# Attention and a gated MLP on one core: the opening of the program is put into another order, its first products are split by head block, and five scalings move to GpSimd

## The chip, the core and the metric

The kernel runs on one core of one Trainium2 chip. A core has TensorE (PE, matmuls; its weight loads are shown as PEld), VectorE (DVE), ScalarE (ACT), GpSimd (POOL) and SyncE (SP), each with its own instruction stream, and DMA engines that move data between the chip's main memory and SBUF, the working memory on the core. Matmuls write to PSUM, eight banks of 128 partitions by 512 float32 values. The metric is the device time of one execution in microseconds (us); lower is better.

## What is computed

```
# x [8, 8, 512, 64], state [8, 8, 32, 64]: batch, heads, rows, depth
scores  = softmax(x @ state^T / 8)          # 512 x 32 for each batch and head
xread   = scores @ state                    # 512 x 64
scores2 = softmax(state @ x^T / 8)          # 32 x 512
sread   = scores2 @ x                       # 32 x 64
X = concat([xread, sread], rows) -> [8 * 544, 512]      # the heads side by side
out = (relu(X @ w_gate) * (X @ w_val)) @ w_out          # 512 -> 1536 -> 512
```

All inputs and the output are float32; the kernel multiplies in bfloat16. It doesn't form xread. Since xread @ w = answers @ (state @ w), it works out U = state @ w once for each batch, for the gate and the value weights, and multiplies the normalized answers (512 by 256 for a batch, heads and state rows side by side, in two head blocks of 128) with U.

## The kernel before, in words

**Pieces of work.** A batch has a number b (0 to 7), and its 1,536 hidden columns are 12 pieces jf of 128. For a batch the steps are: cast of x to bfloat16 and transposes on TensorE (`x_T`, L162) with copies out of PSUM (`x_out`, L165); scores with the state (`att_sc`, L179), exponentials on ScalarE (`att_exp`, L206), row sums and reciprocals on VectorE (`att_sum`, L212 and L214), the scaling a = e * (1 / sum) (`att_scale`, L218), the transposes of a (`att_T`, L234) and their copies (`att_out`, L248), each for head block 0 and 1. U is built in units: `c_unit` (L298, for batches 0 and 1, 128 or 256 columns of gate and value together) or `u_unit` (512 columns of one of them), and cast into SBUF (`c_out` L320, `u_out` L310). A product `gv` (L325) of one piece jf is four matmuls of 512 columns: gate and value, each summed over the two head blocks in one PSUM bank. `relu` (L354, ScalarE) and `mult` (L358, VectorE) make the hidden piece h, and the output matmuls (L367) sum the 12 pieces of h with w_out. The sread rows go through `sr_mm`, `gvs` and `fin_s`.

**Order.** The scheduler of the framework is off (`manual_schedule`, L412): every engine runs its instructions in the order in which the code names them. Up to piece 28 (all 12 pieces of batches 0 and 1, the first four of batch 2) the order is a written list, the string `program` (L455): each word is a step with its arguments, digits behind @ are the PSUM banks that it takes, and a last part act, dve or pool is the engine of a copy, cast or scaling. From piece 28 on a loop (L554) sets one piece of a product and one piece of an output row block in turn, with further work at fixed places. Only the list is in question here; the loop is the same in both kernels.

**Words of the list.** dw and dx load weights and x, ds the state, do the output weights, all on GpSimd's queue. spin and spin32 are matmuls on constants into a bank that nobody reads, in bfloat16 and float32; they keep TensorE busy while it has nothing to do. stc, stT and sto cast, transpose and copy the state; xc casts the half of the first x that is loaded as float32; xT and xo are transposes and copies; sc, ex, nr, nx, aT, ao the attention steps; c and co (u and uo) U's units and casts; gv a whole product, re and mu relu and multiplication; xp copies x into a padded tile for the sread rows. Words ga, gb, wa and wb (one matmul of a product: gate or value, head block 0 or 1) and gg and gw (gate alone, value alone) are defined and not used.

**Queues.** GpSimd's loads use eight semaphores in turn, so the ninth load is issued only when the first has landed. A load stands in GpSimd's stream like any other of its instructions; it is issued when what stands ahead of it is done. Two small loads at the start go out on SyncE's and ScalarE's queues (L420 and L99).

Of the kernel before, what the change touches and what calls it, by code (L numbers as in the profile page):

```python
# [16 lines left out]
def kernel(  # L17
# [9 lines left out]
    nc = tc.nc  # L27

    B, H, S, D = x.shape
# [34 lines left out]
    xa = const.tile([128, NX, NC * H, DP], BF16, name="xa")  # L64
# [4 lines left out]
    stT = const.tile([128, 2, B, H, Ns], BF16, name="stT")  # L69
# [4 lines left out]
    warm32 = nc.const_aps.tensor(1.0, (128, 512), FP32)  # L74
# [3 lines left out]
    xf, xb, xT, eT, e_sn, a_sn, ANS, U, hsb = {}, {}, {}, {}, {}, {}, {}, {}, {}  # L78
# [359 lines left out]
    def spin(n, cols=512, src=warm):  # L438
        for i in range(n):
            nc.tensor.matmul(warm_ps[:, 0:cols], src[:, 0:128], src[:, 0:cols], start=True, stop=True)  # L440
# [3 lines left out]
    def x_load_behind(b, gb, gj):  # L444
# [1 line left out]
        nc.gpsimd.tensor_copy(out=mark, in_=held["g", gb, gj][:, 0:1])  # L446
        x_load(b, 0, 1)

    steps = {"spin32": lambda n: spin(n, 512, warm32), "dxb": x_load_behind, "spin": spin, "stc": state_conv, "stT": state_T, "sto": state_out, "xc": x_conv_pair, "xT": x_T, "on": lambda: nc.gpsimd.memset(xa[:, :, :, D:D + 1], 1.0), "dw": w_load, "dx": x_load, "ds": lambda: state_dma(nc.gpsimd, 2, B), "do": wo_dma,
             "xo": x_out,   # L450
             "sc": att_sc, "ex": att_exp, "nr": att_sum, "nx": att_scale, "aT2": att_T2, "ao2": att_out2, "aT": att_T, "ao": att_out,
             "c": c_unit, "co": c_out, "u": u_unit, "uo": u_out, "gv": gv, "gg": lambda b, jf: g_part(b, jf, 0, (0, 1)), "gw": lambda b, jf: g_part(b, jf, 1, (0, 1)),
             "ga": lambda b, jf: g_part(b, jf, 0, (0,)), "gb": lambda b, jf: g_part(b, jf, 0, (1,)), "wa": lambda b, jf: g_part(b, jf, 1, (0,)), "wb": lambda b, jf: g_part(b, jf, 1, (1,)), "re": relu, "mu": mult, "o": out_part,
             "of": fin_x, "xd": x_trans_dma, "ad": att_aT_dma, "xp": x_pad, "sr": lambda b: sr_mm((b,)), "sn": lambda b: sr_norm((b,))}
# [10 lines left out]
    nx.1.1 aT.1.0@4 aT.1.1@6 c.0.256.256@01 co.1.0.128.0.dve ao.1.0.dve c.1.256.256@57 co.0.256.256.0.act  # L465
    co.1.256.256.0.act co.1.256.256.1.act ao.1.1.dve co.0.256.256.1.dve gv.1.0@46 re.1.0 mu.0.0 mu.0.1 gv.0.2@01
    gv.1.2@53 mu.1.0 re.0.2 c.0.512.256@72 c.1.512.256@40 re.1.2 mu.1.2 co.0.512.256.1.dve mu.0.2 gv.1.3@65
    gv.1.1@32 co.1.512.256.1.act re.1.3 co.0.512.256.0.act re.1.1 co.1.512.256.0.dve gv.0.3@06 gv.1.5@17 mu.1.1
    mu.1.3 re.0.3 re.1.5 gv.1.4@34 mu.0.3 c.0.768.256@02 re.1.4 mu.1.5 c.0.1024.256@51 c.1.768.256@63
    co.0.768.256.0.act co.0.768.256.1.act mu.1.4 co.1.768.256.1.dve co.1.768.256.0.dve gv.0.4@74 gv.0.6@02 re.0.4  # L470
    co.0.1024.256.0.act re.0.6 gv.0.7@37 co.0.1024.256.1.dve mu.0.4 re.0.7 mu.0.6 gv.1.7@65 mu.0.7 re.1.7
    c.0.1280.256@10 c.1.1024.256@43 c.1.1280.256@26 mu.1.7 co.1.1280.256.1.act co.0.1280.256.0.act
    co.0.1280.256.1.dve co.1.1024.256.1.act co.1.1280.256.0.dve gv.0.9@75 co.1.1024.256.0.act gv.0.8@60 gv.0.5@12
    re.0.5 re.0.9 xT.2.0.8@3 re.0.8 mu.0.5 xT.2.8.8@4 xo.2.0.8.dve stT.1@1 sto.1.1.act xo.2.8.8.dve sto.1.0.act
    gv.0.11@72 re.0.11 mu.0.11 mu.0.8 gv.1.9@63 gv.1.11@41 re.1.9 mu.1.9 gv.0.10@76 gv.1.6@20 re.1.11 re.0.10
    sc.2.1@4 gv.1.10@73 re.1.10 ex.2.1 re.1.6 mu.0.10 mu.0.9 o.0.3@6 sc.2.0@5 o.0.4 ex.2.0 o.0.0@7 mu.1.10 mu.1.11
    u.2.1.1024@43 mu.1.6 nr.2.1 uo.2.1.1024.1.act u.2.1.0@21 u.2.1.512@50 uo.2.1.512.1.act uo.2.1.1024.0.act
    uo.2.1.512.0.act uo.2.1.0.0.act nx.2.1 uo.2.1.0.1.dve o.0.1 o.0.5 stc.2.1.pool dx.3.0.1 xp.1 xp.0 sr.1@3
    stc.3.0.pool nr.2.0 sr.0@0 nx.2.0 sn.1 u.2.0.0@14 ad.2 xd.3 of.0.1.act u.2.0.1024@52 u.2.0.512@63 o.0.2 of.0.0.act
    uo.2.0.0.0.act uo.2.0.512.1.act uo.2.0.512.0.dve o.0.6@6 o.0.7 o.0.9@7 o.0.8 of.0.2.act sn.0 gv.1.8@01  # L480
    uo.2.0.0.1.dve uo.2.0.1024.0.dve gv.2.0@45 re.1.8 mu.1.8 re.2.0 mu.2.0 dxb.4.2.0 gv.2.2@36 xp.3 gv.2.3@40 re.2.2 mu.2.2 re.2.3 mu.2.3 xp.2
    gv.2.1@31 re.2.1 mu.2.1 uo.2.0.1024.1.act
    """
    for word in program.split():
        word, _, banks = word.partition("@")
# [117 lines left out]
```

## Time and profile before

| | us |
|---|---|
| time, median of 3 runs | 220.07 (219.66 to 220.4) |
| the profiled execution's own time | 219.39 |
| its span in the profile | 217.6 |
| TensorE busy | 212.8 |
| VectorE busy | 135.0 |
| ScalarE busy | 117.8 |
| GpSimd busy | 42.5 |

The span is the time from the first to the last instruction that the profile shows; the rest of the execution's own time lies around it. A busy time says how long an engine had an instruction under way. The chain of work that ended last goes back from the last instruction to what released it, and so on to the start. A line of a timeline gives start and busy time in us, engine, source line, operation, tile written and tiles read, shapes and count, and in brackets how long the engine stood idle before and who ended that.

### The profile page before, as it was taken

Reading aid. Unit: us, or ns where it says so; the run is one execution under the profiler, and the core shown is the slowest. Engines: PE = TensorE matmul, PEld = TensorE weight load, DVE = VectorE, ACT = ScalarE, POOL = GpSimd, SP = SyncE. Lnnn points to the kernel's source line nnn. Section 1 sums busy time; section 2 is a strip of 40 time slices with the busy share of each in tenths; the row PEclk is TensorE's granted clock in tenths of the full one; section 3 lists DMA queues with packets and bytes.
Section 4 is the critical chain, followed back from the end, with each engine's and each line's share of the span. In section 5 each row is a group of like instructions: output and inputs, shape, how many; then the busy total and the mean of one; then the engine's idle time right before and its main releaser. Section 6 shows DMA issues by size and latency. Waiting matters only on the chain.

```text
span 217.6 us, 4865 instructions
## 1 busy us (share of the span) xinstructions
PE 212.8 (98%) x1952; PEld 104.8 (48%) x1952; DVE 135.0 (62%) x233; ACT 117.8 (54%) x225; POOL 42.5 (20%) x63
## 2 busy tenths in 40 slices
PE   8899999999999999999999999999999999999994
PEld 4554454454444444444444444444544445666543
DVE  4799967956887678557966796388745444222100
ACT  4798877747546556455555656454646443333221
POOL 7974049005600531020107000000000000000000
PEclk9999999999999999999999999999999999999999
DMA  7999999579963995919491453131311122222132
GB/s 168 180 196 197 202 221 171 78 139 188 152 175 74 144 186 110 167 52 193 99 148 60 110 134 96 49 99 50 84 28 51 48 48 50 61 56 80 51 96 96
DMA packets 47399, 24.96 MB, mean 115 GB/s; under 512 B 27824, under 2 KB 43056, under 8 KB 47376
## 3 DMA queue, kind: packets, MB, share of 16 engines
q0 software_dynamic: 16896, 9.05, 31.0%
q1 hardware_dynamic: 29584, 14.85, 28.7%
q10 hardware_dynamic: 896, 0.75, 1.3%
q8 instruction: 15, 0.25, 0.4%
q14 instruction: 8, 0.07, 0.2%
HBM read 18.35 MB, written 8.91 MB: 125 GB/s over the span
## 4 chain that ended last, share of the span: by engine, by line
PE 96%; DVE 1%; ACT 1%; issue 0%
PE o_ps L367 40%; PE gv_ps L325 38%; PE gv_ps L347 5%; PE up L298 4%; PE warm_ps L440 2%; PE upc L298 2%; PE o_ps L396 1%; PE sr_ps L265 1%; PE sc_ps L179 1%; PE sT_ps L189 1%; PE xT_ps L162 1%; ACT e_sn L206 1%; DVE xT L165 1%; ACT xT L165 0%; PE aT_ps L234 0%; DVE cs L212 0%
## 5 line engine op out<-in xcount | busy, mean ns | idle before, releaser
L367 PE MATMUL o_ps<-wo_sb,h_sb 128*128 128x512 bf16 x372 | 94.3, 379 | 0.0
L325 PE MATMUL gv_ps<-ans,U 128*128 128x512 bf16 x384 | 93.2, 379 | 0.0
L358 DVE TENSOR_TENSOR h_sb<-gv_ps,g_sb 128x512 bf16<-128x512 f32 x96 | 65.1, 688 | 42.8 <-ACT g_sb L354 41.3
L354 ACT ACTIVATE g_sb<-gv_ps 128x512 bf16<-128x512 f32 (+1 forms) x108 | 61.7, 578 | 51.4 <-PE gv_ps L325 39.1
L325 PEld LDWEIGHTS <-U 128*128 128x128 bf16 x384 | 37.1, 98 | 44.5 <-issue 0.8
L367 PEld LDWEIGHTS <-h_sb 128*128 128x128 bf16 x372 | 35.2, 98 | 42.0 <-issue 4.0
L310 DVE CAST U<-up 128x512 bf16<-128x512 f32 x44 | 27.7, 684 | 5.7 <-PE up L298 5.7
L375 ACT COPY o_sb<-o_ps 128x512 f32<-128x512 f32 x31 | 18.4, 594 | 19.7 <-PE o_ps L367 17.7
L310 ACT CAST U<-up 128x512 bf16<-128x512 f32 x28 | 14.7, 595 | 8.8 <-PE up L298 8.8
L254 POOL COPY xa<-xb 128x1024 bf16<-128x1024 bf16 x16 | 16.0, 1045 | 10.0 <-PE sr_ps L265 5.9
L358 DVE TENSOR_TENSOR hs_sb<-gv_ps,g_sb 128x256 bf16<-128x256 f32 x12 | 5.1, 425 | 15.3 <-PE gv_ps L347 10.4
L212 DVE TENSOR_REDUCE cs<-e_sn 128x16 f32<-128x512 bf16 x16 | 10.8, 677 | 1.1 <-ACT e_sn L206 1.1
L218 DVE TENSOR_TENSOR a_sn<-e_sn,rc 128x512 bf16<-128x512 bf16 x16 | 10.9, 687 | 0.4
L298 PEld LDWEIGHTS <-stT 64*32 64x32 bf16 x560 | 6.7, 91 | 6.4 <-issue 5.3
L320 ACT CAST U<-upc 128x512 bf16<-128x512 f32 (+1 forms) x19 | 8.7, 522 | 1.7 <-PE upc L298 1.7
L446 POOL COPY mark<-g_sb 128x1 bf16<-128x1 bf16 x4 | 0.8, 190 | 41.8 <-ACT g_sb L354 41.8
L197 ACT ACTIVATE eT<-sT_ps 128x512 bf16<-128x512 f32 x10 | 5.4, 594 | 5.3 <-PE sT_ps L189 5.3
L434 POOL DMA_DIRECT2D xb<-in_x_dram x8 | 6.8, 847 | 3.1 <-DMA wg_sb<-in_moe_w_gate_dram 1.4
L347 PE MATMUL gv_ps<-br,wg_sb 128*128 128x256 bf16 x48 | 7.2, 273 | 0.0
L347 PE MATMUL gv_ps<-br,wv_sb 128*128 128x256 bf16 x48 | 7.2, 273 | 0.0
L399 DVE COPY o_sb<-o_ps 128x64 f32<-128x64 f32 x2 | 0.4, 224 | 10.6 <-PE o_ps L396 10.5
L298 PE MATMUL up<-wg_sb,stT 64*32 64x512 bf16 (+1 forms) x168 | 6.9, 348 | 0.0
(59 smaller groups left out, 124.1 us busy)
## 6 DMA issues: line engine op xcount, KB each, us to landing
out_dram<-o_sb SPq DMA_DIRECT2D x26, 256.0 KB, 2.4
xb<-in_x_dram POOLq DMA_DIRECT2D x6, 512.0 KB, 7.1
wo_sb<-in_moe_w_out_dram POOLq DMA_DIRECT2D x2, 768.0 KB, 10.5
out_dram<-o_sb SPq DMA_DIRECT2D x11, 128.0 KB, 2.4
wg_sb<-in_moe_w_gate_dram POOLq DMA_DIRECT2D x5, 256.0 KB, 9.4
wv_sb<-in_moe_w_val_dram POOLq DMA_DIRECT2D x5, 256.0 KB, 10.0
xb<-in_x_dram POOLq DMA_DIRECT2D x3, 256.0 KB, 5.3
st_f<-in_state_dram POOLq DMA_DIRECT2D x1, 384.0 KB, 11.4
```

The costliest lines, as they stand in the source:

```text
L212: nc.vector.reduce_sum(out=cs, in_=e_v, axis=AX.X)
L218: {"dve": nc.vector, "pool": nc.gpsimd}[eng].tensor_tensor(out=a_sn[b][:, jp].rearrange("p c (j n) -> p c j n", n=Ns), in0=e_v, in1=held[" ...
L254: nc.gpsimd.tensor_copy(out=v[:, hs], in_=xb[b][:, hs])
L298: nc.tensor.matmul(dst[kc][i0:i0 + 32], stT[r:r + 64, parity, b, h], wsb[r:r + 64, j, lo:lo + n], start=True, stop=True)
L310: copy[eng](out=U[b][:, w, kc, lo:lo + 512], in_=held["u", b, w, lo][kc])
L320: copy[eng](out=U[b][:, :, kc, lo:lo + n], in_=held["c", b, lo][kc])
L325: nc.tensor.matmul(ps[w], U[b][:, w, kc, f0:f0 + 128], ANS[b][:, kc].rearrange("p c t -> p (c t)"), start=(kc == 0), stop=(kc == NK - 1))
L347: nc.tensor.matmul(ps[w][:, 0:nt], wsb[:, j, f0:f0 + 128], br[:, j].rearrange("p b n -> p (b n)"), start=(j == 0), stop=(j == NJ - 1))
L354: nc.scalar.activation(out=g_sb[:, 0:n], in_=ps[0][:, 0:n], func=AF.Relu)
L358: nc.vector.tensor_tensor(out=dst, in0=ps[1][:, 0:n], in1=held["g", b, jf][:, 0:n], op=ALU.mult)
L367: nc.tensor.matmul(held["o", b, tsub], src[:, jf, tsub * 128:(tsub + 1) * 128], wo_sb[:, jf], start=(jf == 0), stop=(jf == NF - 1))
L375: copy[eng](out=o_sb, in_=held["o", b, tsub])
```

## The change

Almost all of it is the list. Its new order issues the same computation, with these differences:

- The first product matmuls of batches 0 and 1 (pieces 0 to 3) are split into ga, wa, gb and wb, the part over head block 0 ahead of the part over head block 1, with other work between them. The other pieces of the list are split into gg and gw. The number and size of the product matmuls stay the same.
- Five scalings (batch 0, both blocks; batch 1, block 0; batch 2, both blocks) go from VectorE to GpSimd.
- The loads of the weights stand among the other words: the value weights of columns 512 to 767 behind the first two scalings, the further ones behind the third and partly behind the padding copies of batch 1. The order of the loads among themselves stays as it was, but the second half of the output weights now follows the first half directly.
- Fillers: 2 float32 matmuls of 512 columns at the start become one of 512 and one of 320; eight bfloat16 fillers of 128 to 512 columns become six float32 ones of 64 to 512 columns. `spin32` gets a number of columns as second argument.
- Copies and casts change engines in many places: the two casts of the first state pair stand on VectorE and ScalarE instead of both on VectorE, the copies of stT both on VectorE instead of one each.

```diff
-    steps = {"spin32": lambda n: spin(n, 512, warm32), "dxb": x_load_behind, ...
+    steps = {"spin32": lambda n, cols=512: spin(n, cols, warm32), "dxb": x_load_behind, ...
...
     program = """
-    dx.1.0.2 dx.1.1.2 stc.0.1.dve stc.0.0.dve dw.0.0.128 dw.1.0.128 dw.0.128.128 dw.1.128.128 dw.0.256.256
-    dw.1.256.256 dw.0.512.256 spin32.2 stT.0@0 dw.1.512.256 dw.0.768.256 dw.1.768.256 dw.0.1024.256 dw.1.1024.256
-    dw.0.1280.256 dw.1.1280.256 dx.2.0.1 ds do.0.6 xc.0.0.act spin.1.256 xT.0.0.4@1 xc.0.1.dve sto.0.0.act
-    spin.1.128 xT.0.4.4@2 xo.0.0.4.dve sto.0.1.dve xo.0.4.4.act spin.1 sc.0.0@3 ex.0.0 nr.0.0 spin.1.384
-        xT.0.8.4@4 xT.0.12.4@5 xo.0.8.4.act xo.0.12.4.act spin.1 xT.1.0.8@6 sc.0.1@1 ex.0.1 xo.1.0.8.dve spin.1
-    sc.1.0@0 xT.1.8.8@2 stc.1.1.pool stc.1.0.pool do.6.12 spin.1 c.0.0.128@34 nx.0.0 ex.1.0 nr.0.1 xo.1.8.8.act on
-    stc.2.0.pool stc.3.1.pool co.0.0.128.0.act co.0.0.128.1.act spin.1 sc.1.1@5 nx.0.1 nr.1.0 aT.0.1@6 aT.0.0@1
-    ex.1.1 c.1.128.128@02 ao.0.0.dve ao.0.1.act c.0.128.128@34 c.1.0.128@51 co.0.128.128.0.act gv.0.0@63
-    co.1.128.128.1.act co.0.128.128.1.act re.0.0 co.1.128.128.0.act gv.0.1@72 nr.1.1 nx.1.0 co.1.0.128.1.act re.0.1
...
+    dx.1.0.2 dx.1.1.2 stc.0.0.dve stc.0.1.act spin32.1 spin32.1.320 stT.0@0 xc.0.0.dve dw.0.0.128 xT.0.0.4@1
+    sto.0.1.dve xc.0.1.act dw.1.0.128 xo.0.0.4.act spin32.1.320 xT.0.4.4@2 dw.0.128.128 xo.0.4.4.dve sto.0.0.dve
+    dw.1.128.128 spin32.1 sc.0.0@0 dw.0.256.256 xT.0.8.4@2 ex.0.0 xT.0.12.4@1 xo.0.8.4.dve dw.1.256.256
+    xo.0.12.4.dve nr.0.0 spin32.1.416 sc.0.1@1 dw.0.512.256 xT.1.0.8@2 ex.0.1 nx.0.0.pool xo.1.0.8.act nr.0.1
+    spin32.1.352 xT.1.8.8@1 xo.1.8.8.dve spin32.1.64 sc.1.0@2 nx.0.1.pool aT.0.0@0 ex.1.0 ao.0.0.dve spin32.1.64
+    c.0.0.128@13 sc.1.1@4 nr.1.0 dw.1.512.256 co.0.0.128.0.act aT.0.1@0 ex.1.1 c.1.0.128@25 ga.0.0@1
+    co.0.0.128.1.dve ao.0.1.act wa.0.0@6 nx.1.0.pool nr.1.1 c.0.128.128@47 c.1.128.128@03 co.0.128.128.0.act
+    wb.0.0 co.0.128.128.1.act gb.0.0 dw.0.768.256 co.1.0.128.1.dve wa.0.1@4 co.1.128.128.0.act aT.1.0@7 nx.1.1
+    re.0.0 ga.0.1@5 dw.1.768.256 gb.0.1 co.1.0.128.0.act ao.1.0.dve wb.0.1 aT.1.1@1 re.0.1 mu.0.0 xp.1 ga.1.1@7
...
```

The rest of the list, up to piece 28, is in a new order of the same kind.

More of the change, by code (lines that the diff above doesn't have):

```diff
@@ L447, in x_load_behind @@
         x_load(b, 0, 1)
-    steps = {"spin32": lambda n: spin(n, 512, warm32), "dxb": x_load_behind, "spin": spin, "stc": state_conv, "stT": state_T, "sto": state_out, "xc": x_conv_pair, "xT": x_T, "on": lambda: nc.gpsimd.memset(xa[:, :, :, D:D + 1], 1.0), "dw": w_load, "dx": x_load, "ds": lambda: state_dma(nc.gpsimd, 2, B), "do": wo_dma,
+    steps = {"spin32": lambda n, cols=512: spin(n, cols, warm32), "dxb": x_load_behind, "spin": spin, "stc": state_conv, "stT": state_T, "sto": state_out, "xc": x_conv_pair, "xT": x_T, "on": lambda: nc.gpsimd.memset(xa[:, :, :, D:D + 1], 1.0), "dw": w_load, "dx": x_load, "ds": lambda: state_dma(nc.gpsimd, 2, B), "do": wo_dma,
              "xo": x_out,
@@ L466 @@
[L466 to L480, printed above, removed]
@@ new lines @@
+    wa.0.2@5 co.1.512.256.0.dve re.0.2 wa.1.2@6 ds wb.1.2 wa.0.3@0 co.1.512.256.1.act mu.1.2 wb.0.3 do.0.6 wb.0.2
+    co.0.512.256.0.act c.0.768.256@21 mu.0.3 c.1.768.256@63 do.6.12 gg.1.4@7 co.0.768.256.0.dve co.1.768.256.1.act
+    gg.0.5@0 xp.0 re.1.4 mu.1.1 gw.1.4@3 co.1.768.256.0.act gg.1.5@2 mu.0.2 re.0.5 gw.0.5@4 co.0.768.256.1.dve
+    re.1.5 c.0.1024.256@56 c.1.1024.256@07 co.0.1024.256.0.dve co.0.1024.256.1.act gg.1.7@1 gw.0.4@2
+    co.1.1024.256.1.dve re.1.7 gg.0.4@5 co.1.1024.256.0.act mu.1.4 gw.1.7@1 gg.0.7@7 mu.1.7 gw.0.7@3 re.0.7 mu.0.5
@@ new lines @@
+    gg.0.6@0 re.0.4 c.1.1280.256@71 mu.0.7 c.0.1280.256@46 co.1.1280.256.1.act gw.0.6@5 mu.0.4 re.0.6 gg.0.8@3
+    co.0.1280.256.1.dve gw.1.5@2 co.1.1280.256.0.act gg.1.8@0 co.0.1280.256.0.dve gg.0.9@7 mu.1.5 stc.2.1.pool
+    gg.0.10@4 stc.1.0.pool re.0.9 mu.0.6 gg.1.6@6 stc.2.0.pool re.0.8 stc.1.1.pool gw.0.8@7 stc.3.1.pool re.1.8
+    xT.2.0.8@5 dx.3.0.1 re.0.10 stT.1@3 gw.0.10@0 sto.1.0.act on gg.0.11@4 mu.0.10 stc.3.0.pool gw.1.10@2
+    xo.2.0.8.dve gg.1.9@1 re.1.6 gw.0.11@0 mu.0.8 sto.1.1.act gg.1.10@6 re.0.11 gw.1.8@7 gw.0.9@3 mu.0.11
@@ L483 @@
+    of.0.2.act gg.2.0@0 mu.1.11 gg.2.2@5 re.2.0 uo.2.0.512.0.dve gg.2.3@6 uo.2.0.1024.0.act gw.2.2@0 dxb.4.2.0
+    gg.2.1@1 gw.2.1@2 xp.3 re.2.1 o.0.2 re.2.3 mu.2.1 gw.2.0@1 of.0.0.act gw.2.3@2 re.2.2 o.0.9@7 mu.2.3 mu.2.0
+    mu.2.2
     """
```

12 lines of the change are left out of this document (9 added, 3 removed).

## Prediction

> **What bounds the kernel now.** I read the page's busy table first, then its chain of work that ended last, then the timeline of each engine up to 20 us.
>
> From the page (busy us and share, then the chain by engine):
>
> ```profile
> PE 212.8 (98%) x1952; PEld 104.8 (48%) x1952; DVE 135.0 (62%) x233; ACT 117.8 (54%) x225; POOL 42.5 (20%) x63
> ...
> PE 96%; DVE 1%; ACT 1%; issue 0%
> ```
>
> TensorE bounds it. Its mathematics is the same in both kernels, so only three things can move the end: filler matmuls (spins) that run when real work could, waits of TensorE, and matmuls at the lower clock. All of these lie ahead of the first product of answers and U, at 13.01 us; behind it the timeline shows TensorE busy in every slice.
>
> TensorE's timeline (start, busy, what; in brackets the idle time before):
>
> ```profile
> 0.78 3.75 PE L440 MATMUL warm_ps<-const-float32-1.0 128*128 128x512 f32 x4 [0.78 <-PEq L587]
> 4.32 0.63 PE L123 MATMUL stT_ps<-id,st_b 128*128 128x128 bf16 x4
> 4.96 0.63 PE L162 MATMUL xT_ps<-id,xb 128*128 128x128 bf16 x4
> 5.50 0.53 PE L162 MATMUL xT_ps<-id,xb 128*128 128x128 bf16 x4
> 6.57 0.43 PE L179 MATMUL sc_ps<-stT,xT 128*128 128x64 bf16 x8 [0.33 <-DVE stT L140]
> 7.97 0.62 PE L162 MATMUL xT_ps<-id,xb 128*128 128x128 bf16 x8
> 9.41 0.41 PE L179 MATMUL sc_ps<-stT,xT 128*128 128x64 bf16 x8 [0.26 <-DVE xT L165]
> 13.01 1.90 PE L325 MATMUL gv_ps<-ans,U 128*128 128x512 bf16 x8
> ```
>
> Four transposes took 0.63 us at 4.96, eight took 0.62 at 7.97: with some 0.2 of drain in each, one took 0.107 early and 0.056 later. The clock doubled at about 5.75. The float32 filler costs 3.54 us for 1,024 columns at the low clock (0.78 to 4.32), 3.4 ns a column; I take 1.7 ns behind 5.75.
>
> VectorE's, ScalarE's and GpSimd's timelines:
>
> ```profile
> 5.63 0.42 DVE L165 COPY xT<-xT_ps 128x512 bf16<-128x512 bf16 x1 [0.46 <-PE xT_ps L162]
> 7.66 0.69 DVE L212 TENSOR_REDUCE cs<-e_sn 128x16 f32<-128x512 bf16 x1 [1.15 <-ACT e_sn L206]
> 9.27 0.68 DVE L218 TENSOR_TENSOR a_sn<-e_sn,rc 128x512 bf16<-128x512 bf16 x1
> ```
>
> ```profile
> 4.01 0.62 ACT L144 CAST xb<-xf 128x512 bf16<-128x512 f32 x1 [0.84 <-DMA xf<-in_x_dram]
> 10.35 1.01 ACT L165 COPY xT<-xT_ps 128x1024 bf16<-128x1024 bf16 x1
> ```
>
> ```profile
> 9.54 0.74 POOL L109 DMA_DIRECT2D wv_sb<-in_moe_w_val_dram  x1 [0.18 <-issue]
> 30.09 0.73 POOL L118 CAST st_b<-st_f 128x256 bf16<-128x256 f32 x2 [9.27 <-DMA st_f<-in_state_dram]
> 33.70 3.98 POOL L254 COPY xa<-xb 128x1024 bf16<-128x1024 bf16 x4
> ```
>
> The prices: VectorE copies 0.42, reduction 0.69, scaling 0.68; a ScalarE copy of 1,024 columns 1.01; GpSimd 1.0 ns an element in bf16 copies (3.98 for four of 1,024) and 1.4 in casts that read float32 (0.73 for two of 256).
>
> **The change, step by step.** Times from the span's start; 0.04 us passes from a producer's end to its consumer (VectorE's copy of stT ended at 6.52, the scores began at 6.57).
>
> *State and first half of x.* 832 filler columns instead of 1,024: 2.88 us, to 3.66. The two casts of the state stand on two engines; the later, ScalarE's (0.38), ends at 3.73. State transposes at 3.78 instead of 4.32. The first cast of x goes to VectorE at 4.01 (0.45); transposes at 4.50 instead of 4.96. Gain so far 0.46.
>
> *The filler of 320 columns.* It runs from 4.93, 0.82 us at the low clock and 0.12 behind the switch, to 5.87. ScalarE's cast of the second half (4.72 to 5.34) lets the next transposes go at 5.39: 0.48 is lost, they start 0.37 later than the old 5.50. They are readable at 6.25.
>
> *Two copies in line on VectorE.* The copy of these transposes (6.29 to 6.71) and that of the second half of stT (to 7.12) both stand on VectorE; ScalarE, which did half of this before, is idle from 5.8. Scores 0.0 at 7.17, 0.60 later. The 512-column filler (0.85, to 6.94) is hidden under this.
>
> *First scaling.* Exponentials 7.63 to 8.23; the two transposes behind the scores are now both copied on VectorE (7.86 to 8.62) ahead of the reduction, which runs 8.60 to 9.28 instead of at 7.66; reciprocal to 9.56; GpSimd from 9.60.
>
> *The price of a GpSimd scaling* of 512 elements is not in the trace of before. Lower bound 0.52, one input at the copy's rate; upper bound 1.4, both inputs at the rate of the float32 casts (1,024 x 1.4). I take 1.2, between the copy that reads as many elements (1.05) and the upper end, because one of the inputs is float32. The Trainium skill (GPSIMD Engine Reference, Elementwise — side-by-side cycle accounting) has about 2.6 cycles an element for two inputs, an estimate of 1.1 us here, and the sum by it would be the same.
>
> *To the first product.* Scaling 0.0 ends at 10.80. TensorE's own line: scores 0.1 at 8.67 (the second copy), transposes of batch 1 to 9.37, filler 352 (0.59) to 9.96, transposes to 10.41, filler 0.11. Scores 1.0 wait for ScalarE, whose copy of 1,024 runs behind the exponentials, 9.64 to 10.65: they start at 10.70 instead of 9.41. Answer transposes 10.95; the first U unit needs the bank that VectorE copies until 11.42; scores 1.1 to 11.83. The second scaling runs 10.80 to 12.0, its transposes 12.05 to 12.27, a unit of 0.12: first product at 12.39, 0.62 earlier than before. Two U units (0.24) that before had then done are still to come: at equal work TensorE is 0.38 **ahead**. The split by head block does this, as the first products need only the first block's answers.
>
> *Behind it.* The split holds two banks for each product open, and banks are where TensorE now waits. The U unit of batch 1 wants bank 0, which ScalarE empties only behind the exponentials of 1.1 (12.0 to 12.6) and the 0.60 copy: about 0.33 of wait near 13.0. Product 0.1 wants bank 5, which VectorE empties behind a reduction, a reciprocal and another cast: 0.27 near 14.3. Batch 1's products want its answers, copied until 15.4: 0.08; one more of 0.06. In sum 0.74. From 16 us on VectorE and ScalarE are nearly full, as the table by stretches shows (stretch, length, busy of PE, PEld, DVE, ACT, POOL):
>
> ```profile
> 13.00:36.00 23.00, 23.00 (x284) 11.51 (x274) 20.00 (x35) 19.66 (x40) 10.16 (x17) 1.00 1.33 199
> ```
>
> 20.00 and 19.66 of 23 us; I add 0.15 for further short bank waits, between 0 and 0.4.
>
> *The queue on GpSimd.* The scalings wait for VectorE, and behind them stand the loads: the value weights of column 512 are issued at 12.0 instead of 9.54, those of 768 at about 14 and 14.7, and behind two copies of 1.05 those of 1024 at 17.8 instead of 11.75. Loads land one behind the other, 1.33 us each (the one issued at 9.54 landed 8.8 later, the one at 15.14 11.2 later, six steps in 8.0 us), so the queue is never empty unless a load is issued within its own latency, 5.2 to 5.8 us for the first ones. At worst the weights of 1024 land by 23.6, wanted at 25; the output weights by 34.5, wanted at 37.8. Cost nothing; if the cover were gone, about 1 us.
>
> *VectorE* is rid of five scalings, 0.6 each; three lie before 15 us and are already in the walk. The two of batch 2 lie near 38 us, beside output products that don't wait for them: nothing.
>
> Sum: -0.38 + 0.74 + 0.15 = **+0.5 us**. The profiled execution took 219.39 (span 217.6, 1.79 outside it), so 219.9 in its conditions; the median of the runs, 220.07, stands 0.68 above it, and with the same step it becomes **220.6**.
>
> **The rivals.**
>
> *Late loads.* In the profiled execution the transposes of batch 1 (7.97) and the value weights (landed 10.7, used at 10.75) had no slack, so each 0.1 us of later loads costs the old kernel 0.1. The new order wants them at 8.92 and 11.5, with 0.8 to spare. If the 0.68 by which the median stands above the profiled run is loads, the new kernel does not pay it: 219.9, no change. Against it: what lies outside the span may also vary.
>
> *The bank waits don't come.* If ScalarE is 0.35 earlier at the exponentials of 1.1, 0.6 of the 0.74 goes: 220.0, and with late loads 219.3, **faster**. It decides at the wait for bank 0 near 13 us.
>
> *The GpSimd scaling is over 1.35 us.* Then the transposes of both blocks of batch 0 and the first of batch 1 wait for it, 0.3 for each 0.1: at 1.6 us 221.4, **slower**. Against it: only the casts' rate for both inputs goes that far.
>
> *The clock rises later.* The new fillers are float32 and sit on the path: were the clock low until 7.6 us, the filler of 512 would cost 0.85 more and the short ones 0.2, of which 0.45 lies under copies, so 221.2, **slower**. For it: the new order leaves TensorE idle from 4.21 to 4.50, where the old one was busy throughout. The Trainium skill (TensorE: Matmul & The Clock Gate, What's actually happening) says that the gate opens after a busy window of about 3.4 us that runs free of the kernel's start; by that rule the switch falls anywhere between 4.2 and 7.6 us, and the one trace here, with 5.75, agrees but cannot show the spread.
>
> **How the numbers follow.** This kernel's runs (219.66 to 220.4) tell no change below about 0.3%, 0.66 us. Chances: the sum as worked out 0.38 (0.26 within 0.3%, 0.12 slower, as 220.6 is near the bound of 220.73); late loads 0.20 (0.15 within, 0.05 faster); no bank waits 0.14 (0.07 faster, 0.07 within); scaling too long 0.13, clock 0.15, both slower. Faster 0.12, same 0.48, slower 0.40. The range runs from 219.4, late loads with half the bank waits, to 221.9, a scaling of 1.75 us; the likeliest case's own is 220.1 to 221.1.
>
> **What would show it.** Right: first product near 12.4 us; scores 0.0 near 7.2; GpSimd TENSOR_TENSOR rows of 1.05 to 1.35; TensorE waits named by ScalarE and VectorE between 12.7 and 15.5; no wait for weights; span near 218.1. Wrong: scalings over 1.35, early transposes at 0.107 behind 6 us, or no waits around 13 us.

## The result, and the profile after

| | before | after |
|---|---|---|
| time, median of 13 runs each, us | 219.96 (219.18 to 220.4) | 220.86 (220.23 to 221.02) |
| ratio, with its 95% interval | | 1.0035 [1.0021, 1.0049] |
| the profiled execution's own time | 219.39 | 220.58 |
| its span | 217.6 | 218.8 |

The changed kernel is slower by 0.9 us in the medians and by 1.2 in the two profiled executions, a small loss, but a real one: the interval of the ratio lies above 1 (the two medians alone give 1.0041). The prediction had 220.6 with a range of 219.4 to 221.9; the loss that it forecast was 0.5, the measured one 0.9.

The page's busy table and its chain of work that ended last, of the kernel after:

```profile
PE 211.4 (97%) x1931; PEld 104.9 (48%) x1956; DVE 134.7 (62%) x233; ACT 115.2 (53%) x220; POOL 48.0 (22%) x68
...
PE 93%; ACT 2%; issue 2%; DMA 1%; DVE 1%; DVEq 0%; ACTq 0%
```

TensorE still bounds the kernel; the five scalings show on GpSimd, which is busy 5.5 us more (48.0 against 42.5). Behind the written list the loss is constant: of the 62 VectorE multiplications between 66 us and 183, all but four come 1.14 to 1.25 us later than in the kernel before, most of them 1.17 (the four by 1.4 to 1.6, and the next ones are back at 1.14 to 1.24). So all of it arises in the opening. TensorE's timeline there (start, busy, what, idle before):

```profile
4.01 0.61 PE L123 MATMUL stT_ps<-id,st_b 128*128 128x128 bf16 x4
4.64 0.61 PE L162 MATMUL xT_ps<-id,xb 128*128 128x128 bf16 x4
5.86 0.38 PE L162 MATMUL xT_ps<-id,xb 128*128 128x128 bf16 x4
7.17 0.39 PE L179 MATMUL sc_ps<-stT,xT 128*128 128x64 bf16 x8
...
12.48 0.39 PE L325 MATMUL gv_ps<-ans,U 128*128 128x512 bf16 x1
13.02 0.25 PE L298 MATMUL upc<-wg_sb,stT 64*32 64x128 bf16 x8
...
14.11 0.39 PE L234 MATMUL aT_ps<-id,a_sn 128*128 128x128 bf16 x4
14.33 0.81 PE L325 MATMUL gv_ps<-ans,U 128*128 128x512 bf16 x3
15.62 0.40 PE L234 MATMUL aT_ps<-id,a_sn 128*128 128x128 bf16 x4 [0.47 <-ACT g_sb L354]
15.95 0.81 PE L325 MATMUL gv_ps<-ans,U 128*128 128x512 bf16 x3
16.69 0.30 PE L298 MATMUL upc<-wg_sb,stT 64*32 64x256 bf16 x8
```

The first scores (7.17) and the first product (12.48) stand within 0.1 us of where the prediction put them. The three products at 14.33 are over at 14.98 (0.216 each, without the drain); then TensorE has nothing until the last transposes of answers at 15.62. The row puts the end of that wait down to ScalarE; the view of waits of the weight loads, in which the answers are the stationary operand, names the scaling (total, times, longest):

```profile
PEld L234 <- DVE a_sn L218: 1.0, 1, 1.0
```

That scaling is the one of batch 1 that stayed on VectorE. VectorE's and GpSimd's timelines:

```profile
14.02 1.54 DVE L218 TENSOR_TENSOR a_sn<-e_sn,rc 128x512 bf16<-128x512 bf16 x1
```

```profile
9.62 2.24 POOL L218 TENSOR_TENSOR a_sn<-e_sn,rc 128x512 bf16<-128x512 bf16 x2
...
12.83 1.04 POOL L218 TENSOR_TENSOR a_sn<-e_sn,rc 128x512 bf16<-128x512 bf16 x1 [0.22 <-ACT e_sn L206]
13.82 0.80 POOL L109 DMA_DIRECT2D wg_sb<-in_moe_w_gate_dram  x1
14.62 0.75 POOL L109 DMA_DIRECT2D wv_sb<-in_moe_w_val_dram  x1
15.36 2.08 POOL L254 COPY xa<-xb 128x1024 bf16<-128x1024 bf16 x2
```

It took 1.54 us. In the kernel before, the two scalings of batch 1 took 1.22 together, 0.61 each; this is their row, and TensorE's first U unit of 256 columns there:

```profile
13.53 1.22 DVE L218 TENSOR_TENSOR a_sn<-e_sn,rc 128x512 bf16<-128x512 bf16 x2
```

```profile
15.28 0.30 PE L298 MATMUL upc<-wg_sb,stT 64*32 64x256 bf16 x8
```

Nothing in the prediction had the long scaling; the experiments turn on it.

**Where the time went.** Count the work by the list (a few matmul records are missing from the traces): at 16.69 us the kernel after begins its first U unit of 256 columns, with 11 product matmuls and four units done; the one before did so at 15.28 with 8 products. Three products are 0.65 us, so after stands at 16.04 against 15.28: 0.76 behind. At the first product it was 0.29 ahead (12.48 against 13.01, less two U units of 0.12 that before had already done). So 1.05 is lost between 12.5 and 16.7 us, of which 0.64 is the wait for the last answers. The other 0.41 of the loop's 1.17 comes behind it: at 25.43 (42 products and ten units, against 40 and eight at 23.52 before, at 0.216 and 0.23 each) the same count gives 1.0 behind, and there the new list changes between products and U units twice where the old one does so once.

### The profile page after: what moved, and what is told of

It is laid out like the page before. It is cut to its first block, busy times and chain, and to the rows that moved or that the text cites. A ratio compares the mean times of both kernels' runs of the same rounds, so it can differ in the third digit from the quotient of the medians.

```text
span 218.8 us, 4838 instructions
## 1 busy us (share of the span) xinstructions
PE 211.4 (97%) x1931; PEld 104.9 (48%) x1956; DVE 134.7 (62%) x233; ACT 115.2 (53%) x220; POOL 48.0 (22%) x68
## 4 chain that ended last, share of the span: by engine, by line
PE 93%; ACT 2%; issue 2%; DMA 1%; DVE 1%; DVEq 0%; ACTq 0%
PE o_ps L367 39%; PE gv_ps L325 36%; PE gv_ps L347 5%; PE up L298 4%; PE upc L298 2%; PE warm_ps L440 2%; DMA st_f<-in_state_dram 1%; PE o_ps L396 1%; PE xT_ps L162 1%; PE sr_ps L265 1%; ACT g_sb L354 1%; DVE h_sb L358 1%; PE sT_ps L189 1%; PE sc_ps L179 1%; ACT U L320 1%
## 5 line engine op out<-in xcount | busy, mean ns | idle before, releaser
L367 PE MATMUL o_ps<-wo_sb,h_sb 128*128 128x512 bf16 x355 | 91.1, 379 | 2.4 <-issue 2.1
L354 ACT ACTIVATE g_sb<-gv_ps 128x512 bf16<-128x512 f32 (+1 forms) x108 | 60.9, 579 | 52.3 <-PE gv_ps L325 39.3
L320 ACT CAST U<-upc 128x512 bf16<-128x512 f32 (+1 forms) x16 | 7.7, 510 | 2.5 <-PE upc L298 2.3
L218 DVE TENSOR_TENSOR a_sn<-e_sn,rc 128x512 bf16<-128x512 bf16 x11 | 8.5, 769 | 0.4
L440 PE MATMUL warm_ps<-const-float32-1.0 128*128 128x512 f32 (+4 forms) x16 | 7.7, 580 | 0.8 <-PEq L591 0.8
L320 DVE CAST U<-upc 128x512 bf16<-128x512 f32 (+1 forms) x12 | 7.2, 629 | 0.1
L218 POOL TENSOR_TENSOR a_sn<-e_sn,rc 128x512 bf16<-128x512 bf16 x5 | 5.2, 1044 | 9.2 <-DVE rc L214 8.8
```

The lines of the kernel that those rows point to most:

```text
L218: {"dve": nc.vector, "pool": nc.gpsimd}[eng].tensor_tensor(out=a_sn[b][:, jp].rearrange("p c (j n) -> p c j n", n=Ns), in0=e_v, in1=held[" ...
L320: copy[eng](out=U[b][:, :, kc, lo:lo + n], in_=held["c", b, lo][kc])
L354: nc.scalar.activation(out=g_sb[:, 0:n], in_=ps[0][:, 0:n], func=AF.Relu)
L367: nc.tensor.matmul(held["o", b, tsub], src[:, jf, tsub * 128:(tsub + 1) * 128], wo_sb[:, jf], start=(jf == 0), stop=(jf == NF - 1))
```

## The experiments

Each kernel is compared with runs of the kernel before taken beside it; a ratio below 1.0035 is better than the kernel after. The kernel after was not run beside them, so its interval, 1.0021 to 1.0049, belongs in each such comparison. All compute the whole result.

| kernel | median, us | before beside it | ratio to before |
|---|---|---|---|
| e_quiet: nothing on GpSimd beside the long scaling | 221.3 | 220.12 | 1.0043 [1.0024, 1.0062] |
| e_loads_behind: padding copies beside it | 221.67 | 220.12 | 1.0069 [1.0049, 1.0090] |
| e_scal_dve: all five scalings on VectorE | 223.27 | 220.12 | 1.0195 [1.0147, 1.0243] |
| e_nofill320: without one filler | 221.57 | 220.12 | 1.0068 [1.0048, 1.0088] |
| e_quiet_xp: as e_quiet, padding copies late | 220.10 | 219.82 | 1.0012 [0.9992, 1.0033] |
| v_only_sto: state copied on ScalarE | 220.36 | 219.82 | 1.0028 [1.0016, 1.0039] |
| e_late_before: before, with later loads | 221.33 | 219.82 | 1.0080 [1.0057, 1.0102] |
| e_late_after: after, with later loads | 221.54 | 219.82 | 1.0078 [1.0061, 1.0095] |
| e_unsplit: products not split | 221.66 | 219.87 | 1.0086 [1.0052, 1.0120] |
| v_c1: e_quiet_xp and v_only_sto | 220.01 | 219.87 | 1.0006 [0.9986, 1.0027] |
| v_c7: v_c1, batch 1 scaled on GpSimd | 220.61 | 219.87 | 1.0030 [1.0001, 1.0058] |
| v_c8: v_c1, batch 1 scaled on VectorE, loads early | 220.5 | 219.96 | 1.0023 [1.0008, 1.0038] |

### The long scaling (e_quiet, e_loads_behind, e_quiet_xp)

`qt` is a copy of one column on GpSimd that waits for the scaling, so that the loads of columns 768 go out behind it:

```diff
-    ... gb.0.0 dw.0.768.256 co.1.0.128.1.dve wa.0.1@4 co.1.128.128.0.act aT.1.0@7 nx.1.1
-    re.0.0 ga.0.1@5 dw.1.768.256 gb.0.1 ...
+    ... gb.0.0 co.1.0.128.1.dve wa.0.1@4 co.1.128.128.0.act aT.1.0@7 nx.1.1 qt.1.1 dw.0.768.256
+    re.0.0 ga.0.1@5 dw.1.768.256 gb.0.1 ...
```

> The new order, with GpSimd kept still while VectorE does the one scaling that stayed with it (batch 1, block 1): the two load issues that ran beside it now wait until it is done. Theory A (GpSimd's work behind its own scaling holds that VectorE scaling, 1.54 us instead of 0.69, and the answers of batch 1 wait for it): the scaling falls back to 0.69, the second transposes of batch 1 start near 15.1 instead of 15.62, and the time falls by 0.5 to 0.9 from 220.86, to about 220.1, no longer to be told from before. Rival B (the long scaling is a freak of one execution, or its delay is taken up later): 220.7 to 221.0, ratio to before 1.003 to 1.005.

VectorE's and then TensorE's timeline of e_quiet:

```profile
14.34 0.67 DVE L218 TENSOR_TENSOR a_sn<-e_sn,rc 128x512 bf16<-128x512 bf16 x1
```

```profile
34.40 0.40 PE L123 MATMUL stT_ps<-id,st_b 128*128 128x128 bf16 x4 [1.05 <-POOL st_b L118]
```

With GpSimd idle beside it the scaling takes 0.67, although it starts 0.15 behind the end of a GpSimd scaling, as the long one does; so a GpSimd scaling that is over doesn't hold it. And TensorE gains: by the relu instructions this execution is 0.32 us behind the kernel after at 14 us, ahead of the scaling, and 0.42 ahead of it from 18 to 33, 0.74 in all. But the loads of 768 are issued 1.5 us later (15.31 instead of 13.82), the state of the next batches, further back in the same queue, lands at 32.85 instead of 30.44, and TensorE waits 1.05 for its cast. The gain is paid back there, and more. The runs of e_quiet lie in two groups, five at 220.1 to 220.7 and seven at 221.3 to 222.1; the profiled one, with the wait, is of the second.

The second kernel changes what stands beside the scaling: the two loads move behind the padding copies (`xp.1`), so a GpSimd copy runs beside it instead of a load issue.

```diff
-    ... gb.0.0 dw.0.768.256 co.1.0.128.1.dve ... ga.0.1@5 dw.1.768.256 gb.0.1 ... mu.0.0 xp.1 ga.1.1@7
+    ... gb.0.0 co.1.0.128.1.dve ... ga.0.1@5 gb.0.1 ... mu.0.0 xp.1 dw.0.768.256 dw.1.768.256 ga.1.1@7
```

> The new order with the two load issues and the two padding copies on GpSimd exchanged, so that copies that read SBUF, not load issues, follow GpSimd's third scaling and run beside VectorE's scaling. If reading SBUF on GpSimd is what holds a VectorE operation with two SBUF inputs, the scaling takes 1.0 to 1.7 us again, and the time stays at 220.7 to 221.0. If only issuing loads behind a GpSimd scaling does it, the scaling takes 0.69 and the time is near 220.1. The loads land at most 1 us later and are not waited for.

VectorE, GpSimd and TensorE of e_loads_behind:

```profile
14.10 1.38 DVE L218 TENSOR_TENSOR a_sn<-e_sn,rc 128x512 bf16<-128x512 bf16 x1
```

```profile
13.90 2.48 POOL L254 COPY xa<-xb 128x1024 bf16<-128x1024 bf16 x2
```

```profile
34.81 0.40 PE L123 MATMUL stT_ps<-id,st_b 128*128 128x128 bf16 x4 [0.98 <-POOL st_b L118]
```

Beside the copies the scaling takes 1.38: it starts 0.2 behind the first copy and ends about 0.6 behind that copy's end (14.93), so it ran when the copy was over, and the two copies take 2.48 together instead of 2.08, the second one 1.50. The two take turns, whole instructions at a time. The Trainium skill (SBUF — State Buffer, Who interferes with whom) says so: a VectorE instruction with two inputs in SBUF and a GpSimd instruction that reads SBUF want the same read port, one has it to its end and the other stands still. The trace agrees, 1.38 against 0.68. The section counts no load issue among the holders, though, and in the kernel after it is issues that stand beside the 1.54; v_c8 comes back to this. The expectation that these loads are not waited for was missed: they go out 2.5 us later than in the kernel after (16.33 against 13.82), and the state behind them, itself issued only 0.5 later, lands 2.8 later (33.26), so that TensorE waits for it.

The third kernel keeps `qt` and gives the queue its time back, by moving the padding copies from ahead of the next loads to a place further back in the list, beside those of batch 0, where nobody waits for them:

```diff
     ... nx.1.1 qt.1.1 dw.0.768.256 re.0.0 ga.0.1@5 dw.1.768.256 ...
-    ... re.0.1 mu.0.0 xp.1 ga.1.1@7
+    ... re.0.1 mu.0.0 ga.1.1@7
...
-    gg.0.5@0 xp.0 re.1.4 ...
+    gg.0.5@0 xp.1 xp.0 re.1.4 ...
```

> The new order with GpSimd still beside VectorE's scaling, as in the run before, and the two padding copies of batch 1 moved behind the last weight load, so that the loads behind it are not late. Theory A (the long scaling costs the end about 0.7 us; what took this away again in the run before was the state of batches 2 and 3, landing too late for its transposes): scaling 0.69, no wait ahead of the state transposes near 33 us, 220.0 to 220.4. Rival B (the end does not follow the scaling): 220.7 to 221.0 with the same two rows.

VectorE and TensorE of e_quiet_xp:

```profile
14.45 0.68 DVE L218 TENSOR_TENSOR a_sn<-e_sn,rc 128x512 bf16<-128x512 bf16 x1
```

```profile
33.29 0.39 PE L123 MATMUL stT_ps<-id,st_b 128*128 128x128 bf16 x4
```

The scaling takes 0.68 and there is no wait for the state. The ratio falls from 1.0035 to 1.0012: by it, about 0.5 of the 0.9 us of loss is the long scaling. The intervals of the two ratios overlap, so this size is rough. The traces give it more narrowly: by the relu instructions at 14 and 18 us, as for e_quiet, this kernel gains 0.75 on the kernel after and v_c1 gains 0.74, while v_only_sto, which keeps the long scaling, gains nothing there. Here the gain is kept to the end.

### Scalings, split and filler, each undone (e_scal_dve, e_unsplit, e_nofill320)

All five scalings go back to VectorE, with the rest of the new list kept:

```diff
-    ... nx.0.0.pool ... nx.0.1.pool ... nx.1.0.pool ... nx.2.1.pool ... nx.2.0.pool ...
+    ... nx.0.0 ... nx.0.1 ... nx.1.0 ... nx.2.1 ... nx.2.0 ...
```

> The new order with all five scalings back on VectorE, in the places where the words stand. Theory A (in this order VectorE is what the opening waits for, so the scalings on GpSimd carry the gain of the split): slower by 1.5 to 2.5 us than the new kernel, 222.4 to 223.4; the scalings take 0.69 each, the long one too. Rival B (GpSimd's scalings, 1.05 against 0.69 us, are no gain): 220.0 to 220.9.

VectorE, GpSimd and TensorE of e_scal_dve:

```profile
11.06 0.68 DVE L218 TENSOR_TENSOR a_sn<-e_sn,rc 128x512 bf16<-128x512 bf16 x1
...
13.14 1.43 DVE L218 TENSOR_TENSOR a_sn<-e_sn,rc 128x512 bf16<-128x512 bf16 x1
```

```profile
11.24 0.76 POOL L109 DMA_DIRECT2D wv_sb<-in_moe_w_val_dram  x1
11.97 2.05 POOL L254 COPY xa<-xb 128x1024 bf16<-128x1024 bf16 x2
```

```profile
14.63 0.40 PE L234 MATMUL aT_ps<-id,a_sn 128*128 128x128 bf16 x4 [0.25 <-DVE a_sn L218]
15.79 0.81 PE L325 MATMUL gv_ps<-ans,U 128*128 128x512 bf16 x3 [0.76 <-DVE U L320]
```

The scaling at 11.06, beside a load issue, took 0.68; the one at 13.14, beside a padding copy, 1.43. VectorE is then late with the cast of U that product 0.1 wants, and TensorE waits 0.76 for it. The span is 221.0, 2.2 us over the kernel after: with the words where they stand, the new order needs its scalings on GpSimd. The six runs spread from 222.83 to 226.04, so the ratio is rough; the medians give 1.0143. That the long scaling would take 0.69 here was expected and missed: a padding copy stands beside it now.

The products of the first four pieces become whole words again, each where the part over the second head block stood:

```diff
-    ... ga.0.0@1 ... wa.0.0@6 ... wb.0.0 ... gb.0.0 ... wa.0.1@4 ... ga.0.1@5 ... gb.0.1 ... wb.0.1 ...
+    ... gw.0.0@6 ... gg.0.0@1 ... gg.0.1@5 ... gw.0.1@4 ...
```

> The changed list with the products of the first four pieces no longer split by head block: gate and value of a piece are four matmuls in two words as in the pieces behind them, each at the place where the second block's part stood. My theory (the split by head block gives the 0.38 of head start, and the bank waits are its price): first products at 13.4 to 13.6 instead of 12.48, less waiting for banks 0 and 5, together about 0.5 slower than the changed kernel, 221.3 us, ratio 1.006. Rival (the split buys nothing since the waits for banks and for the long scaling set the time at 15.6 us anyway): ratio 1.0035 as the changed kernel, TensorE's idle time between 12 and 16 us the same in sum. Rival (the open banks are the loss): faster than the changed kernel, 1.002.

TensorE's timeline of e_unsplit:

```profile
12.46 0.25 PE L298 MATMUL upc<-wg_sb,stT 64*32 64x128 bf16 x8 [0.19 <-ACT e_sn L206]
...
12.93 0.25 PE L298 MATMUL upc<-wg_sb,stT 64*32 64x128 bf16 x8 [0.17 <-ACT ans L248]
...
13.39 0.81 PE L325 MATMUL gv_ps<-ans,U 128*128 128x512 bf16 x3 [0.16 <-issue]
```

The first product comes at 13.39, although the first scores of this execution were 0.28 earlier than in the kernel after (6.89 against 7.17), and TensorE now waits for the banks with nothing to put in between. The ratio is 1.0086, 1.1 us more than the kernel after, so the split does gain. The 0.5 of the expectation (ratio 1.006) still lies within its wide interval.

The filler of 320 columns ahead of the second half of the x transposes is left out:

```diff
-    ... xo.0.0.4.act spin32.1.320 xT.0.4.4@2 ...
+    ... xo.0.0.4.act xT.0.4.4@2 ...
```

> The new order without the float32 filler of 320 columns ahead of the second transposes of batch 0. Theory A (the filler lies on the path): those transposes start near 5.4 instead of 5.86, scores 0.0 near 6.7 instead of 7.17, and 0.2 to 0.4 us of it reach the end: 220.5 to 220.65. Rival B (another wait ends last, such as the second half of x or the reduction): 220.8 to 220.9. Rival C (the filler is what raises the clock in time): transposes at 0.107 behind 6 us, 221.2 or more.

TensorE's timeline of e_nofill320:

```profile
5.51 0.61 PE L162 MATMUL xT_ps<-id,xb 128*128 128x128 bf16 x4 [0.28 <-ACT xb L144]
...
7.72 0.64 PE L179 MATMUL sc_ps<-stT,xT 128*128 128x64 bf16 x8
8.16 1.04 PE L162 MATMUL xT_ps<-id,xb 128*128 128x128 bf16 x8
...
14.00 0.39 PE L325 MATMUL gv_ps<-ans,U 128*128 128x512 bf16 x1
```

The transposes come 0.35 earlier (5.51 against 5.86), as the prediction's 0.37 has it, and it is a loss: eight transposes at 8.16 take 1.04 where the kernel after needs 0.61 at 7.40, so the clock is still low, and the first product is 1.5 later. In this execution the filler pays for itself by raising the clock. No other one of this kernel was traced; the six runs, 220.91 to 222.06, agree with a loss.

### Two copies in line, and late loads (v_only_sto, e_late_before, e_late_after)

The second copy of stT goes to ScalarE, and the filler beside it is cut to 256 columns:

```diff
-    ... xo.0.4.4.dve sto.0.0.dve dw.1.128.128 spin32.1 sc.0.0@0 ...
+    ... xo.0.4.4.dve sto.0.0.act dw.1.128.128 spin32.1.256 sc.0.0@0 ...
```

> The new order with the second half of the copies of stT on ScalarE, which is idle then, instead of behind another copy on VectorE, and the filler beside it cut from 512 to 256 columns. By the walk of the prediction the scores of batch 0 begin 0.4 us earlier, near 6.75, and with them the chain to the first product. Theory A (that chain sets the end): 0.3 to 0.5 us below 220.86, so 220.4 to 220.55. Rival B (loads of batch 1 or the banks behind the first product end last): 220.8 to 220.9. Rival C (the shorter filler leaves TensorE too idle for its clock): transposes at 0.107 behind 7 us, over 221.2.

The first scores came at 6.84 instead of 7.17 and the first product at 12.24 instead of 12.48; the scaling still took 1.54 and the last transposes of answers came at 15.37. In its trace the kernel stays 0.25 ahead of the kernel after to the end. The ratio moves from 1.0035 to 1.0028, which the intervals don't separate.

One more load of 256 KB, which nobody reads, is set first on GpSimd's queue, so that each later load lands later:

```diff
+    nc.gpsimd.dma_start(out=spare[:, 1024:2048].rearrange("p (f m) -> p f m", f=2), in_=moe_w_out[0:256]...)
```

> The kernel before with one more load of 256 KB, which nobody uses, ahead of all loads on GpSimd's queue, so that x of batches 0 (second half) and 1 and all weights land about 1.35 us later. Theory (late loads cost the old order their whole lateness, as it has no slack): 1.2 to 1.4 us slower, 221.2 to 221.5. Rival (other waits hide some of it): under 0.8.

> The new order with the same extra load. Theory (it has 0.8 to 0.9 us of slack in the transposes of batch 1 and the first weights): slower by 0.4 to 0.6 than the new order alone, 221.2 to 221.5, as fast as the old order with the extra load. Rival (the new order gains nothing under late loads): 1.2 to 1.4 slower, 222.1.

The first products of e_late_before and of e_late_after:

```profile
14.12 1.90 PE L325 MATMUL gv_ps<-ans,U 128*128 128x512 bf16 x7
```

```profile
8.84 0.62 PE L162 MATMUL xT_ps<-id,xb 128*128 128x128 bf16 x8 [1.60 <-DMA xb<-in_x_dram]
...
13.97 0.39 PE L325 MATMUL gv_ps<-ans,U 128*128 128x512 bf16 x1
```

The old order loses 1.8 us by its ratio, the new one 0.9 (1.0078 against 1.0035), and the two kernels are then equal. By the ratios, then, late loads cost the new order about half of what they cost the old one, but the difference is hardly clear of the intervals, and the traces don't show it: x lands 1.2 later in e_late_before than in the kernel before, and the first product is 1.1 later; it lands 1.6 later in e_late_after than in the kernel after, and the first product is 1.5 later. The wait of 1.60 in the new order is for the second half of the first x, which in the kernel after landed at 7.20 and was used at 7.40: there is no slack of 0.8 there.

### Looking for a version that beats both (v_c1, v_c7, v_c8)

v_c1 has the edits of e_quiet_xp and v_only_sto together.

> The changed list with both mends at once: the last scaling of batch 1 runs beside nothing on GpSimd (a small copy on GpSimd waits for it, the loads of columns 768 stand behind that, the padding copies of batch 1 behind piece 8), and the second half of the first state pair is copied by ScalarE, with a filler of 256 instead of 512 columns ahead of the first scores. My theory (the long scaling costs about 0.5 us, the two copies in line on VectorE 0.15, and they lie at different places, so they add): 0.65 below the changed kernel, a ratio to before of 1.0005, 219.9 to 220.1 us, first scores near 6.9, scaling 0.68. Rival (the waits for banks 0 and 5 near 12.4 and 13.7 take back what the earlier scores give): ratio 1.0012 as with the first mend alone. Rival that the late loads of 768 are what is left of the loss: a wait of TensorE named by the weights between 20 and 28 us.

1.0006: as if the two gains added up (the intervals, 0.002 to either side, are too wide to show it), and the kernel is then not told from the one before. In its profiled execution it ran 0.53 ahead of the kernel after until 25 us and then gave that back to a load. TensorE's timeline of v_c1:

```profile
25.53 0.30 PE L298 MATMUL upc<-wv_sb,stT 64*32 64x256 bf16 x8 [0.33 <-DMA wv_sb<-in_moe_w_val_dram]
```

The value weights of columns 1024 are issued 0.66 earlier than in the kernel after (17.46 against 18.12), but those of 768, ahead of them, 1.4 later, and the loads that follow land up to 2.5 us apart instead of 1.33: those weights land at 25.49 instead of 23.99. Between 16 and 22 us the DMA engines move 138 to 161 GB/s here, against 191 to 198 in the kernel after: the queue is not kept full. v_c7 puts the last scaling of batch 1 on GpSimd as well and needs no `qt`:

```diff
-    ... nx.1.1 qt.1.1 dw.0.768.256 ...
+    ... nx.1.1.pool dw.0.768.256 ...
```

> As the kernel with both mends, but the last scaling of batch 1 goes to GpSimd too, directly behind the other one of batch 1, in place of the waiting copy; the loads of 768 stand behind it, as they did behind the waiting copy. My theory (VectorE's scaling is held only by what GpSimd does beside it): on GpSimd it takes 1.05, from about 13.9 to 14.95, the last transposes of answers come at 15.0 instead of 15.3, VectorE has 0.68 less to do at its fullest place, the loads of 768 go out 0.4 earlier: 0.2 to 0.4 below the kernel with both mends, a ratio to before of 0.999 to 0.9995. Rival (TensorE has other work at 15 us, so the answers' time doesn't matter): the same as the kernel with both mends, 1.0005. Rival (other VectorE work with two inputs in SBUF is held instead): a VectorE row of over 1.3 us between 13.9 and 15.

GpSimd and TensorE of v_c7:

```profile
12.68 2.19 POOL L218 TENSOR_TENSOR a_sn<-e_sn,rc 128x512 bf16<-128x512 bf16 x2 [0.21 <-ACT e_sn L206]
14.81 0.81 POOL L109 DMA_DIRECT2D wg_sb<-in_moe_w_gate_dram  x1
```

```profile
14.93 0.40 PE L234 MATMUL aT_ps<-id,a_sn 128*128 128x128 bf16 x4
15.16 0.81 PE L325 MATMUL gv_ps<-ans,U 128*128 128x512 bf16 x3
```

The profiled execution is the shortest of all those of the new order: span 217.9, no wait for weights, 0.79 ahead of the kernel after from 18 us on, though its state transposes started 0.44 later (4.45 against 4.01). But its runs lie in two groups, five at 219.5 to 219.7 and seven at 220.6 to 222.4, and the median is 220.6, so the ratio expected, 0.999 to 0.9995, was missed. In the profiled one (219.72, so of the lower group) the value weights of 1024 land at 24.48 and are used at 24.77; a load 0.3 later makes TensorE wait. That this is what the other seven runs pay was argued and not shown, since no trace of one of them was taken.

v_c8 issues these loads early instead. Both scalings of batch 1 are on VectorE, the second U cast between them:

```diff
-    ... nx.1.0.pool nr.1.1 ... co.1.0.128.1.dve ... nx.1.1 qt.1.1 dw.0.768.256 ...
+    ... nx.1.0 co.1.0.128.1.dve nr.1.1 ... nx.1.1 dw.0.768.256 ...
```

> As the kernel with both mends, but both scalings of batch 1 on VectorE again (the first ahead of the second U cast of batch 1 and the second row sums, the other one behind), so that GpSimd has the two scalings of batch 0 alone and issues the loads of 768 and 1024 right behind them, from about 12.4 us (15.2 in the kernel with both mends, 14.8 with all of batch 1 on GpSimd); padding copies of batch 1 late as there. My theory (the runs above 220.5 us of those two kernels wait for weights or for the state that went out too late, and VectorE's scaling is held by what a GpSimd scaling ahead of the load issue leaves behind): both VectorE scalings take 0.68 although loads are issued beside them; last transposes of answers near 15.2; no wait of TensorE for weights or state; all but one or two of the runs between 219.3 and 220.2, median 219.6 to 219.8, ratio to before 0.9985 to 0.9998. Rival (the long runs come from the clock's rise, which differs between executions, not from the loads): the same two groups of runs as with all of batch 1 on GpSimd, median above 220.2. Rival on the scaling (a load issue beside it holds it by itself at this place): a row of over 1.3 us between 13 and 15.5, answers 0.7 later, ratio 1.003.

VectorE, GpSimd and TensorE of v_c8:

```profile
12.96 0.68 DVE L218 TENSOR_TENSOR a_sn<-e_sn,rc 128x512 bf16<-128x512 bf16 x1
...
14.88 0.69 DVE L218 TENSOR_TENSOR a_sn<-e_sn,rc 128x512 bf16<-128x512 bf16 x1
```

```profile
11.77 0.80 POOL L109 DMA_DIRECT2D wv_sb<-in_moe_w_val_dram  x1
12.57 0.75 POOL L109 DMA_DIRECT2D wg_sb<-in_moe_w_gate_dram  x1
...
14.77 0.78 POOL L109 DMA_DIRECT2D wv_sb<-in_moe_w_val_dram  x1
```

```profile
15.63 0.40 PE L234 MATMUL aT_ps<-id,a_sn 128*128 128x128 bf16 x4 [0.39 <-DVE a_sn L218]
```

Both scalings take 0.68 with loads issued all the while. So an issue doesn't hold the scaling by itself. In the kernel after the scaling begins beside the issue directly behind a GpSimd scaling; here such an issue, at 11.77, has no VectorE scaling beside it. Where it has one, in all five kernels that keep this place of the new order (after, v_only_sto, e_unsplit, e_nofill320, e_late_after), the scaling takes 1.54 every time. How that issue differs stays open. The runs lie closer together (220.16 to 221.02, one group), with the weights of 1024 landed at 24.1 and used from 25.44, which fits the reading of v_c7. My time was missed all the same: VectorE, with two scalings, reaches the second one at 14.88 and the answers are transposed at 15.63, just as late as in the kernel after (15.62), so the 0.8 of v_c7 is gone. What would join v_c7's order to early loads was not found: a load issued ahead of the batch 1 scalings would put each of them 0.75 later on GpSimd. No version here beats the kernel before.

## Why the prediction was right or wrong

The time was 0.26 us over the one predicted and inside the likeliest case's own range (220.1 to 221.1). The ratio, 1.0035, lies where "the same" ends and "slower" begins, the two that held 0.88. The loss was 0.9 us where the sum had 0.5; the median of the kernel before came out at 219.96, not 220.07, and the rest lies in the kernel after. The sum came that near with its terms in partly wrong places:

- **State and first half of x**: 4.01 and 4.64 instead of 3.78 and 4.50. The start of the state transposes differs between executions, 3.84 to 4.45 in those of the new order, so no gain of 0.46 is to be counted on here.
- **The filler of 320 columns**: 5.86 for the 5.87 worked out. The step failed in its reading, "0.48 is lost": without the filler the kernel is slower, and in its trace the clock stays low (e_nofill320).
- **Two copies in line on VectorE**: scores at 7.17, as worked out. What taking it away gains at the end is 0.25 in the trace of v_only_sto and some 0.15 by the ratios, not told from nothing.
- **GpSimd's scaling**: 1.04 to 1.05 us, below the 1.2 I took and nearer to the copy's rate; the estimate of 1.1 by the Trainium skill (GPSIMD Engine Reference, Elementwise — side-by-side cycle accounting) was closer. First product at 12.48 for 12.39: the shorter scalings were taken up by the U unit before it, which takes 0.24 with its two drains and not 0.12. The head start was 0.29 for 0.38.
- **Bank waits of 0.74**: this step failed. Near 13.0 TensorE waited 0.11 (two products from 12.48 end at 12.91, the unit starts at 13.02), not 0.33; near 14.3 it did not wait at all. The wait for batch 1's answers, for which I had 0.08, was 0.64, because VectorE's scaling took 1.54. The 0.74 took its place by chance: two sums of similar size, from different causes, and the time came out right by luck in this term.
- **0.15 for further waits, between 0 and 0.4**: 0.41, so the upper end.
- **The queue, "cost nothing; if the cover were gone, about 1 us"**: both halves held. The kernel after has no wait for weights or state, and issues 1.5 and 2.5 us later cost 1.05 (e_quiet) and 0.98 (e_loads_behind). My landing times were too early, though: the weights of 1024 land at 23.99, not 23.6, and the output weights at 34.70 and 38.51, not by 34.5, both without a wait. And a later issue can delay a landing by more than itself: the state, issued 1.42 later in e_quiet, landed 2.41 later.
- **VectorE, scalings of batch 2: nothing.** No row speaks against it; it wasn't tried alone.

Of the rivals, *late loads* is not settled: the ratios of e_late_before and e_late_after speak for a smaller cost in the new order, their traces don't, and it left out the second half of the first x, which had 0.2 to spare and not 0.8. It didn't set the time: the first loads in the trace of the kernel after land 0.6 later than in that of the kernel before, no load is waited for, and the kernel is slower. *The bank waits don't come* was right on the waits and wrong on the time. *The GpSimd scaling over 1.35 us* is out by the row (1.05). *The clock rises later*: the transposes, 0.61 for four at the low clock and 0.39 at the high one, place the rise anywhere from 3.9 us (0.40 at 3.89 in e_scal_dve) to about 6.6 (0.54 at 6.43 in v_c1) in the kernels that keep the fillers, and between 4.64 and 5.86 in the profiled execution of the kernel after, where it was no part of the loss. What it costs the other runs isn't known; in the trace of e_quiet_xp, where the transposes at 6.14 still took 0.53, the first scores came 0.44 later (7.61). That it differs so between executions agrees with the rule of the Trainium skill (TensorE: Matmul & The Clock Gate, What's actually happening) cited in the prediction, that the window runs free; its earliest place lies a little ahead of the 4.2 that I worked out from it.

## What to carry to other kernels

Moving a two-input instruction to GpSimd isn't only its own price: look at each two-input VectorE instruction that then stands beside GpSimd work, and order the two so that they don't meet. Before shifting loads behind such work, read each load's landing against its use; where the queue was not kept full, later loads were delayed by more than the shift. A filler that seems to stand in the way may be what raises the clock, so take it out only against a run.

## What the runs showed of the hardware that was not expected

- A VectorE scaling with both inputs in SBUF took 0.68 alone and beside load issues (v_c8, e_scal_dve at 11.06), 1.22 to 1.43 beside GpSimd copies (e_loads_behind and, twice, e_scal_dve), and 1.54 where it began beside the load issue directly behind a GpSimd scaling (five kernels). The section of the Trainium skill cited above (SBUF — State Buffer) covers the middle case; the last one it doesn't describe, and what holds it was not settled.
- The same scaling on GpSimd took 1.04 to 1.05 us, but for the first one of some other runs (up to 1.12, in v_c7).
- Without the filler of 320 columns the low clock lasted until behind 9 us (416 columns took 1.32 at 9.00 in e_nofill320, 0.92 at 7.85 in the kernel after).
